# Key-row tiles, job loads and the first denominators re-placed, and TensorE's instructions issued in program order

## The chip, the cores and the metric

The kernel runs on one core of a Trainium2 chip. The metric is the device time of one execution in microseconds (us); for a kernel several executions are timed and the median is used. A core has TensorE (PE, matrix products into eight PSUM banks), VectorE (DVE), ScalarE (ACT), GpSimd (POOL) and SyncE (SP), each with an instruction queue of its own that is worked through in order, and DMA queues; here SyncE issues nearly all loads and GpSimd most stores.

## The reference

x is 2048 x 1024, all in float32. A linear-attention block (32 heads of 32) and a gated MLP are both applied to the normalised x, and the output is x plus one times the silu of the other:

```python
xn = layernorm(x)                                   # 2048 x 1024
q, k, v = xn @ wqkv                                 # 1024 x 3072, 32 heads of 32
phi = lambda t: where(t > 0, t + 1, exp(t)) + 1e-6
kv  = einsum("bhsd,bhse->bhde", phi(k), v);  z = phi(k).sum over tokens
o   = (phi(q) @ kv) / (phi(q) . z + 1e-6)
s   = o.reshape(2048, 1024) @ wo
b   = (silu(xn @ w1) * (xn @ w3)) @ w2              # 1024 -> 3584 -> 1024
out = x + s * silu(b)
```

## The kernel before

Precision comes from splitting every operand into a high and a low part (`split`, L89 to 96: ScalarE writes the high part, L93, VectorE the low one, L94) and three matmuls per product (`mm3`, L98 to 103). A matmul has a 128 x 128 weight tile and 512 columns. All large products use a Strassen-Winograd scheme: seven products (B11, T2, T3, T1, B21, T4, B22, each with a partner on the left: A11, S2, S3, S1, A12, A22, S4) in place of eight, joined by additions of VectorE from PSUM.

The tokens are worked in two halves (`half(h)`, L644). The order of the program is:

- first half: the rows of x are normalised and turned into the left operands (`prepare_first`, `prepare_rest`), then four key gemms, one for each pair of column blocks;
- four query gemms and 28 pairs of gate and up gemms, whose hidden values go to DRAM;
- second half: its left operands are loaded (they were made meanwhile), then four key gemms, the first two of which run product by product side by side (L686); then `row_products` (L548), which multiplies x transposed by the keys of all tokens in 28 steps of two times twelve matmuls, reading x and key rows back from DRAM (x_d, y_d) and leaving four blocks g_d; then the query, gate and up gemms of the second half;
- an attention segment (letter s in tile names) and five layers B0 to B4 of the down projection over 2, 3, 3, 3 and 3 pairs of hidden blocks (letter B in tile names). Each walks over eight groups of tokens. The first group, and the last before another layer, have the block index k outside and the seven products inside, in seven banks at once (`outer`, L1026); while the last group runs, the next layer's operands and weights are split between its k steps. The last layer multiplies by s and adds x (`finish`, L1178).

Side work is cut into small steps in Python generators. A gemm has seven products of twelve matmuls and calls `catch_up` (L412) six times, after a product each. `catch_up` takes first what lies in the list `later` (the turns and sums of key rows, below), and else one step of the first generator in `jobs`. In the first half's query, gate and up gemms this is `next_work` (L781): `prepare_next`, which normalises and turns the second half's rows in four blocks of 27 steps, and then 28 `weight_sums` jobs of three steps, which sum weights of the down projection. With the four steps that `later` takes there are 188 places for 192 steps, and what is left runs at the half's end. In the second half it is `attention_work` (L956): `spread_z` and the `denominators` of the first half's token blocks, then key-value products (`key_values`, L886, from g_d) and their merging with wo (`merge_wo`), then the `divide` jobs (L855), the second half's denominators and more divides. A divide loads queries and reciprocals, lets three steps pass, then multiplies (L873) and makes four sums on VectorE. `go_on` (L817) loads two jobs ahead; all job tiles are of tag "job" in one ring of three places.

A key gemm hands each finished quarter to `use` (L515) in `key_rows`: `phi` (L495 to 499: two ScalarE activations, then one VectorE instruction), and then `later` gets the turn: four transposes of TensorE into a bank (L505) and a copy out by ScalarE (L506). The rows go to pair tiles of the "b" ring (`pb`, eight places), which also holds the split weight products, the splits of the row products and spread z.

No order is written out by hand except where `issue_after` ties an instruction behind another. The framework plans every engine's instruction order from a modelled timeline (L1285): whichever instruction it expects to be ready is put first, on TensorE too, so the order on an engine can differ from that of the program.

Of the kernel before, what the change touches and what calls it, by code (L numbers as in the profile page):

```python
# [16 lines left out]
P = 128  # L17
C = 512
# [4 lines left out]
def tile_linear_attention_times_swiglu(  # L23
# [21 lines left out]


    const = ctx.enter_context(tc.tile_pool(name="const", bufs=1))
    dram = ctx.enter_context(tc.tile_pool(name="dram", bufs=1, space=DRAM))
# [49 lines left out]
    def mm3(acc, w, a, start, stop):  # L98

        (wh, wl), (ah, al) = w, a  # L100
        nc.tensor.matmul(acc, lhsT=wh, rhs=ah, start=start, stop=False, skip_group_check=True)  # L101
        nc.tensor.matmul(acc, lhsT=wh, rhs=al, start=False, stop=False, skip_group_check=True)  # L102
        nc.tensor.matmul(acc, lhsT=wl, rhs=ah, start=False, stop=stop, skip_group_check=True)  # L103

# [15 lines left out]
    def job_tile(shape, name):  # L120
        return praw.tile(shape, F32, tag="job", bufs=3, name=name)

# [98 lines left out]
    def prepare_next(i):  # L221
# [8 lines left out]
        def steps(_):  # L230
# [26 lines left out]
            keep_rows(1, i, "A22", a22)  # L257
            g = st.tile([P, 2, C], F32, tag="xg", bufs=1, name=f"xg{i}")
            nc.gpsimd.tensor_add(out=g[:, 0], in0=a21, in1=a22)
            nc.gpsimd.tensor_sub(out=g[:, 1], in0=a11, in1=a21)  # L260
            yield True
            keep_rows(1, i, "S1", g.rearrange("p n c -> p (n c)"))
            for _ in range(3):
                yield True
            nc.gpsimd.tensor_sub(out=g[:, 0], in0=g[:, 0], in1=a11)
            nc.gpsimd.tensor_sub(out=g[:, 1], in0=a12, in1=g[:, 0])
            yield True
            keep_rows(1, i, "S2", g.rearrange("p n c -> p (n c)"))
            yield True
            p_ = turn("A11", a11)  # L270
            keep("A11", p_)
            nc.scalar.copy(out=a11, in_=p_)
            yield True
            p_ = turn("A21", a21)
            nc.scalar.copy(out=a21, in_=p_)
            yield True
# [234 lines left out]
    def key_rows(h, pair):  # L511
# [12 lines left out]
        def turn(n, c, pk):  # L524
            if (c, n) == (0, 0):
                t = rows[c, n] = small(f"y00_{h}_{pair}")
            else:
                if (1 - c, 1) not in pairs:
                    pairs[1 - c, 1] = pb.tile([P, 2, C], F32, tag="b", name=f"y{c}_{h}_{pair}")
                t = rows[c, n] = pairs[1 - c, 1][:, n if c else 0]  # L530
# [17 lines left out]
    def row_products():  # L548
# [39 lines left out]
        for at, s in enumerate(steps):  # L588
# [15 lines left out]
            for e, (x_, y_) in enumerate(split_.pop(s)):  # L604
                for m in M:
                    c = slice(m * P, (m + 1) * P)
                    mm3(b[m], (x_[:, 0, c], x_[:, 1, c]), (y_[:, 0], y_[:, 1]),
                        begins and e == 0 and not onto, ends and e == 1)
                    if ends and e == 1:
                        row_sums(i, m, b[m], u, v)  # L610
                catch_up()
                yield
# [31 lines left out]
    def half(h):  # L644
# [40 lines left out]
        else:  # L685
            side_by_side(keys(0, paired=True), keys(1, paired=True))  # L686
            for pair in range(2, ND // 2):
                run(keys(pair))
            for _ in row_products():
                pass  # L690
# [125 lines left out]

    def go_on(work):  # L817

        data = [j.load() for j in work[:2]]
        for i, j in enumerate(work):  # L820
            yield from j.steps(data[i])
            if i + 2 < len(work):
                data.append(work[i + 2].load())

# [30 lines left out]
    def divide(m, k):  # L855
# [14 lines left out]
        def steps(t):  # L870
            for _ in range(3):
                yield True
# [80 lines left out]
    def late_work():  # L953
        yield from go_on([divide(m, k) for m in range(LATE, S // (2 * P)) for k in range(ND // 2)])

    def attention_work():  # L956
        yield from spread_z()
        H0, H1 = range(NCH // 2), range(NCH // 2, NCH)
        work = [j for c in H0 for j in denominators(c)]
        for k in range(ND // 2):  # L960
# [4 lines left out]
        work += [divide(m, k) for m in range(NT * H1[0], LATE) for k in range(ND // 2)]  # L965
        yield from go_on(work)

# [321 lines left out]
```

## Time and profile before

| | us |
|---|---|
| median of three runs | 2396.59 |
| lowest, highest | 2396.53, 2399.76 |
| profiled execution | 2399.34 |
| its span | 2397.6 |

| engine | busy us | share of the span |
|---|---|---|
| TensorE, matmuls | 2315.7 | 97% |
| TensorE, weight loads | 1896.1 | 79% |
| VectorE | 1772.2 | 74% |
| ScalarE | 919.6 | 38% |
| GpSimd | 751.0 | 31% |

The span is what the profile covers; the execution's own time is 1.7 us longer. The profiled execution is one of its own, 2.75 us above the median of the timed ones. In the profile's rows PE is a matmul, PEld a weight load that runs beside matmuls, SPq and POOLq are the DMA issues of SyncE and GpSimd. L505 means line 505 of the kernel. A row of the timeline has the start in us, the duration in us, engine, line, operation, written tile <- read tiles, the shape, how many instructions were joined in the row, and in brackets how long the engine had been idle before it and what ended that. A name such as cg__11115 is a bank (a, b, c or d) of a gate (g), key (k), query (q) or up (u) gemm with a number. A row of the waits has the engine's wait, its releaser, and the total, the count and the longest in us.

### The profile page before, as it was taken

To read this page: it belongs to the slowest core of one execution; us is meant where nothing else is said; L and a number is where in the kernel's file an instruction comes from. 1 tells how busy PE (TensorE), PEld (TensorE's weight loads), DVE (VectorE), ACT (ScalarE), POOL (GpSimd) and SP (SyncE) were. 2 spreads that over 40 slices of the span, in tenths; PEclk is the share of its full clock that TensorE was granted. 3 is DMA by queue.
4 is the path that set the end of the run, shared out by engine and by line. 5 is a ranking of instruction groups with operands and counts; after the bars stand their busy time and mean duration, and the time that the engine had idled before them with its cause. 6 is when DMAs were issued, how large, how long until landed. Compare 5 with 4: busy or idle time off the path is not lost.

```text
span 2397.6 us, 30961 instructions
## 1 busy us (share of the span) xinstructions
PE 2315.7 (97%) x10368; PEld 1896.1 (79%) x10368; DVE 1772.2 (74%) x2781; ACT 919.6 (38%) x1639; POOL 751.0 (31%) x892
## 2 busy tenths in 40 slices
PE   6999999999999889999999899999999999999998
PEld 5888788888887778778888788877787888888876
DVE  8878888887887655576766677777855676767798
ACT  5555333433332444344333233223423543342433
POOL 5341534367875320211423434323321000000033
PEclk9999999999999999999999999999999999999999
DMA  6455455476669566754555555557876665766588
GB/s 237 150 171 185 152 177 185 158 227 198 220 226 355 184 195 211 241 176 141 170 169 171 186 178 184 172 166 215 268 235 210 195 208 157 234 201 187 185 262 262
DMA packets 354016, 479.70 MB, mean 200 GB/s; under 512 B 24144, under 2 KB 262736, under 8 KB 353744
## 3 DMA queue, kind: packets, MB, share of 16 engines
q1 hardware_dynamic: 316608, 359.20, 47.8%
q0 software_dynamic: 37248, 118.52, 14.7%
q8 instruction: 81, 1.33, 0.2%
q14 instruction: 79, 0.65, 0.1%
HBM read 308.81 MB, written 172.49 MB: 201 GB/s over the span
## 4 chain that ended last, share of the span: by engine, by line
PE 43%; issue 10%; DMA 7%; DVE 4%; POOL 3%; ACT 1%; SPq 0%; POOLq 0%; DVEq 0%; ACTq 0%
PE g L101 2%; PE g L102 2%; PE g L103 2%; DMA qd<-pq_d 1%; PE cB L101 1%; PE cB L103 1%; PE cB L102 1%; PE aB L101 1%; PE aB L102 1%; PE dB L101 1%; PE aB L103 1%; PE dB L103 1%; PE dB L102 1%; DMA qs_d<-qd 1%; DMA rA22B<-h_d 1%
## 5 line engine op out<-in xcount | busy, mean ns | idle before, releaser
L740 POOL DMA_DIRECT2D h_d<-sg x112 | 82.7, 739 | 272.4 <-DVE sg L736 223.5
L1056 POOL DMA_DIRECT2D u_d<-uB x32 | 17.3, 540 | 407.1 <-DVE uB L1039 381.1
L94 DVE TENSOR_TENSOR xy<-xy,xy 128x512 fp32r<-128x512 f32 x112 | 75.9, 720 | 69.5 <-ACT xy L93 69.2
L93 ACT CAST xy<-xy 128x512 fp32r<-128x512 f32 x112 | 63.9, 620 | 86.2 <-PE g L103 60.1
L102 PE MATMUL g<-xy,xy 128*128 128x512 f32 x224 | 88.5, 395 | 0.0
L103 PE MATMUL g<-xy,xy 128*128 128x512 f32 x224 | 88.1, 394 | 0.0
L101 PE MATMUL g<-xy,xy 128*128 128x512 f32 x224 | 83.0, 395 | 2.8 <-ACT xy L93 2.3
L1039 DVE TENSOR_TENSOR acc<-cB,acc 128x512 f32<-128x512 f32 x50 | 34.3, 687 | 41.0 <-PE cB L103 41.0
L509 POOL DMA_DIRECT2D y_d<-y x40 | 29.7, 751 | 102.5 <-ACT y L506 79.7
L1039 DVE TENSOR_TENSOR acc<-dB,acc 128x512 f32<-128x512 f32 x56 | 38.5, 687 | 29.8 <-PE dB L103 29.6
L877 POOL DMA_DIRECT2D qs_d<-qd x32 | 17.9, 560 | 132.2 <-DVE qd L873 122.2
L722 POOL TENSOR_TENSOR hs<-sg 128x256 f32<-128x256 f32 x56 | 57.0, 1017 | 0.0
L720 POOL TENSOR_TENSOR hs<-hs,sg 128x256 f32<-128x256 f32 x56 | 56.4, 1008 | 0.1
L723 POOL TENSOR_TENSOR hs<-sg,hs 128x256 f32<-128x256 f32 x56 | 55.5, 992 | 1.6
L873 DVE SCALAR_TENSOR_TENSOR qd<-qd 128x512 f32<-128x512 f32 x32 | 21.9, 684 | 42.4 <-DMA qd<-pq_d 42.4
L101 PEld LDWEIGHTS g<-xy,xy 128*128 128x128 f32 x224 | 42.2, 189 | 12.5 <-ACT xy L93 2.9
L719 POOL TENSOR_TENSOR hs<-sg,sg 128x256 f32<-128x256 f32 x56 | 50.0, 892 | 1.2
L698 POOL DMA_DIRECT2D pq_d<-pq x32 | 17.4, 545 | 104.7 <-DVE pq L499 104.7
L102 PEld LDWEIGHTS g<-xy,xy 128*128 128x128 f32 x224 | 42.9, 192 | 9.0
L103 PEld LDWEIGHTS g<-xy,xy 128*128 128x128 f32 x224 | 42.9, 192 | 9.0
L748 POOL DMA_DIRECT2D h_d<-hs x60 | 45.9, 766 | 3.7 <-POOL hs L723 2.1
L755 POOL TENSOR_TENSOR w<-w 128x256 f32<-128x256 f32 x28 | 26.7, 955 | 58.5 <-DMA w<-in_B_w 58.5
(5311 smaller groups left out, 8383.7 us busy)
## 6 DMA issues: line engine op xcount, KB each, us to landing
h_d<-hs POOLq DMA_DIRECT2D x60, 256.0 KB, 3.3
h_d<-sg POOLq DMA_DIRECT2D x56, 256.0 KB, 3.5
w<-in_B_w SPq DMA_DIRECT2D x56, 256.0 KB
wt_d<-w SPq DMA_DIRECT2D x28, 512.0 KB
xy<-x_d SPq DMA_DIRECT2D x28, 512.0 KB
xy<-y_d SPq DMA_DIRECT2D x28, 512.0 KB
h_d<-hs SPq DMA_DIRECT2D x52, 256.0 KB
qs_d<-qd POOLq DMA_DIRECT2D x32, 384.0 KB, 4.6
```

What stands on the lines that cost most here:

```text
L93: nc.scalar.copy(out=hi, in_=src)
L94: return nc.vector.tensor_sub(out=lo, in0=src, in1=hi.bitcast(F32))
L101: nc.tensor.matmul(acc, lhsT=wh, rhs=ah, start=start, stop=False, skip_group_check=True)
L102: nc.tensor.matmul(acc, lhsT=wh, rhs=al, start=False, stop=False, skip_group_check=True)
L103: nc.tensor.matmul(acc, lhsT=wl, rhs=ah, start=False, stop=stop, skip_group_check=True)
L719: e.tensor_add(out=s1, in0=a21, in1=a22)
L720: e.tensor_sub(out=s2, in0=s1, in1=a11)
L722: e.tensor_sub(out=s3, in0=a11, in1=a21)
L723: e.tensor_sub(out=s4, in0=a12, in1=s2)
L740: nc.gpsimd.dma_start(out=h_d[i][2 * h + c][:, 2 * n:4 * n + 2, k], in_=src)
L748: queue.dma_start(out=h_d[i][2 * h + c][:, 6 + 4 * e:10 + 4 * e, k], in_=o[e].rearrange("p (e s) -> p e s", s=P))
L1039: return V.tensor_add(out=c, in0=src, in1=c)
```

## The change

- TensorE is taken out of the planner: `manual_schedule` over the whole kernel makes its instructions issue in the order of the program. The other engines are planned as before.
- The ring of job tiles has four places in place of three. `go_on` takes how many jobs to load ahead; `attention_work` asks for three.
- `prepare_next` turns A21 earlier, in the steps after the first sums, and holds its sums g in the job ring; it has 24 steps in place of 27, in each of four blocks.
- The key rows' pair tiles come from the job ring in place of the b ring.
- In `row_products` what `catch_up` issues is tied behind the last matmul of the twelve before it (for this `mm3` returns its last matmul).
- `spread_z` and the first half's denominators (one and 16 steps) are a job of their own, `first_denominators`, put ahead of the row products, and so run in their steps; `attention_work` begins with the key-value products.
- A divide lets four steps pass in place of three, except for the last two groups of tokens.

```diff
+    ctx.enter_context(tc.manual_schedule(engines={mybir.EngineType.PE}))
     const = ctx.enter_context(tc.tile_pool(name="const", bufs=1))
...
-        nc.tensor.matmul(acc, lhsT=wl, rhs=ah, start=False, stop=stop, skip_group_check=True)
+        return nc.tensor.matmul(acc, lhsT=wl, rhs=ah, start=False, stop=stop, skip_group_check=True)
...
-        return praw.tile(shape, F32, tag="job", bufs=3, name=name)
+        return praw.tile(shape, F32, tag="job", bufs=4, name=name)
...
-            g = st.tile([P, 2, C], F32, tag="xg", bufs=1, name=f"xg{i}")
+            g = job_tile([P, 2, C], f"xg{i}")
             nc.gpsimd.tensor_add(out=g[:, 0], in0=a21, in1=a22)
             nc.gpsimd.tensor_sub(out=g[:, 1], in0=a11, in1=a21)
             yield True
             keep_rows(1, i, "S1", g.rearrange("p n c -> p (n c)"))
-            for _ in range(3):
-                yield True
+            p_ = turn("A21", a21)
+            nc.scalar.copy(out=a21, in_=p_)
+            yield True
+            yield True
             nc.gpsimd.tensor_sub(out=g[:, 0], in0=g[:, 0], in1=a11)
             nc.gpsimd.tensor_sub(out=g[:, 1], in0=a12, in1=g[:, 0])
             yield True
             keep_rows(1, i, "S2", g.rearrange("p n c -> p (n c)"))
-            yield True
             p_ = turn("A11", a11)
             keep("A11", p_)
             nc.scalar.copy(out=a11, in_=p_)
-            yield True
-            p_ = turn("A21", a21)
-            nc.scalar.copy(out=a21, in_=p_)
             yield True
...
-                    pairs[1 - c, 1] = pb.tile([P, 2, C], F32, tag="b", name=f"y{c}_{h}_{pair}")
+                    pairs[1 - c, 1] = job_tile([P, 2, C], f"y{c}_{h}_{pair}")
...
-                    mm3(b[m], (x_[:, 0, c], x_[:, 1, c]), (y_[:, 0], y_[:, 1]),
-                        begins and e == 0 and not onto, ends and e == 1)
+                    last = mm3(b[m], (x_[:, 0, c], x_[:, 1, c]), (y_[:, 0], y_[:, 1]),
+                               begins and e == 0 and not onto, ends and e == 1)
                     if ends and e == 1:
                         row_sums(i, m, b[m], u, v)
-                catch_up()
+                with tc.issue_after(last.ins):
+                    catch_up()
                 yield
...
+            jobs.append((first_denominators(), False))
             for _ in row_products():
                 pass
...
-    def go_on(work):
+    def go_on(work, ahead=2):
 
-        data = [j.load() for j in work[:2]]
+        data = [j.load() for j in work[:ahead]]
         for i, j in enumerate(work):
             yield from j.steps(data[i])
-            if i + 2 < len(work):
-                data.append(work[i + 2].load())
+            if i + ahead < len(work):
+                data.append(work[i + ahead].load())
...
-            for _ in range(3):
+            for _ in range(4 if m < LATE else 3):
                 yield True
...
+    H0, H1 = range(NCH // 2), range(NCH // 2, NCH)
+
+    def first_denominators():
+        yield from spread_z()
+        yield from go_on([j for c in H0 for j in denominators(c)])
+
     def attention_work():
-        yield from spread_z()
-        H0, H1 = range(NCH // 2), range(NCH // 2, NCH)
-        work = [j for c in H0 for j in denominators(c)]
+        work = []
...
-        yield from go_on(work)
+        yield from go_on(work, 3)
```

## The prediction

> **What bounds the kernel now.** I read the page's sums first, then busy time by stage, then TensorE's waits, then the timeline round each.
>
> ```profile
> span 2397.6 us, 30961 instructions
> PE 2315.7 (97%) x10368; PEld 1896.1 (79%) x10368; DVE 1772.2 (74%) x2781; ACT 919.6 (38%) x1639; POOL 751.0 (31%) x892
> ```
>
> TensorE is busy for 97%, so what can be won or lost is its pauses. The stages, in columns of window, length, PE, PEld, DVE, ACT, POOL, granted clock, DMA share and GB/s:
>
> ```profile
> 766.00:862.00 96.00, 83.18 (x387) 67.69 (x386) 59.27 (x107) 43.68 (x79) 33.66 (x38) 0.96 0.59 195
> 862.00:1004.00 142.00, 141.55 (x625) 116.82 (x624) 77.76 (x117) 61.70 (x109) 20.75 (x22) 1.00 0.71 232
> 1004.00:1022.00 18.00, 14.99 (x72) 11.35 (x71) 13.29 (x31) 6.82 (x12) 4.53 (x5) 0.91 0.56 190
> 1340.00:1400.00 60.00, 53.16 (x228) 43.27 (x227) 43.88 (x80) 16.29 (x28) 18.92 (x25) 0.94 0.56 177
> 1840.00:1875.00 35.00, 31.55 (x133) 24.15 (x132) 27.29 (x50) 22.80 (x48) 2.70 (x5) 1.00 0.84 272
> 1875.00:2036.00 161.00, 161.00 (x712) 133.37 (x711) 102.59 (x188) 68.56 (x139) 6.49 (x12) 1.00 0.57 175
> 2036.00:2064.00 28.00, 28.00 (x125) 23.18 (x124) 27.03 (x49) 12.67 (x25) 1.62 (x3) 1.00 0.84 271
> 2265.00:2398.00 133.00, 119.17 (x512) 96.10 (x511) 118.03 (x196) 49.26 (x94) 38.91 (x43) 0.96 0.86 262
> ```
>
> Inside a layer TensorE never pauses: 712 matmuls in 161.00 us, 0.226 us each, which is the pace used below. It pauses in the second half's keys (766 to 862), at the row products' end, at 1374 and at some layer starts. At 2036 it doesn't pause although VectorE is full (27.03 of 28 us). The waits, as total, times, longest:
>
> ```profile
> PE trk L505 <- DVE pk L499: 11.7, 4, 6.7
> PE cg__11115 L101 <- DVE c22g__11150 L462: 6.2, 1, 6.2
> PE g L101 <- ACT xy L93: 2.3, 1, 2.3
> PE bk__6485 L101 <- ACT T2k__6324 L93: 2.0, 1, 2.0
> PE cg__13351 L101 <- DVE c22g__13386 L462: 1.8, 1, 1.8
> ...
> PE aq__8368 L101 <- ACT uq__8367 L439: 0.7, 1, 0.7
> ```
>
> **Gains.** *The divide* (waits one step more, loads three jobs ahead out of four places).
>
> ```profile
> 1363.97 0.69 DVE L873 SCALAR_TENSOR_TENSOR qd<-qd 128x512 f32<-128x512 f32 x1 [7.58 <-DMA qd<-pq_d]
> 1374.01 0.80 PE L101 MATMUL cg__11115<-A,T4g__11153 128*128 128x512 f32 x1 [6.24 <-DVE c22g__11150 L462]
> L101 PE MATMUL cg__11115<-A,T4g__11153 x4: 389/545/796, 1374.0 to 1377.5; 128*128 128x512 f32 x4
> ```
>
> VectorE stands 7.58 us before a divide whose rows haven't landed; behind it in its queue is the sum that frees the bank for cg__11115, and TensorE loses 6.24 us, then some 1.7 in a slow restart (545 ns where steady matmuls have 389). One step more (one product, 12 x 0.226 = 2.7 us) and one job more ahead (five steps, 13.6 us) cover 7.58. With cg__13351's 1.8 this is 9.7: −10. Ends: −11, and −4 if the sixteen later divides meet the same lateness with only the longer wait.
>
> *The row products' end and the first keys of the second half.*
>
> ```profile
> 1007.52 1.52 PE L101 MATMUL g<-xy,xy 128*128 128x512 f32 x4 [2.33 <-ACT xy L93]
> 1008.84 0.63 PE L102 MATMUL g<-xy,xy 128*128 128x512 f32 x1
> 740.97 4.91 SPq L776 DMA_DIRECT2D wt_d<-w  x1
> 760.41 0.50 PE L101 MATMUL bk__6485<-S,T2k__6324 128*128 128x512 f32 x1 [2.04 <-ACT T2k__6324 L93]
> 762.27 0.64 PE L103 MATMUL bk__6485<-S,T2k__6324 128*128 128x512 f32 x1 [1.14 <-DVE T2k__6324 L94]
> ```
>
> In 1004 to 1022, 18.00 − 14.99 = 3 us are lost: the last steps' splits wait behind other work. With the b ring freed of four key-row tiles a pair this can go: −3 (0 to −4). At 740.97 the stores of the left-over weight sums (192 steps for 188 places) still stand in SyncE's queue ahead of the second half's loads. The change's 27 − 24 = 3 steps less, four times, lets all fit (180 for 188): of 2.04 + 1.14 and some 2 of slow restart I take −2.5 (0 to −5). Another 0.7 is the first query gemm's wait for its copy (last line of the waits): ScalarE and VectorE then no longer spread z beside it. Gains: −16 (−5 to −21).
>
> **Losses.** *Key rows in program order.* At present the planner puts the four transposes of a key tile wherever they are ready. In program order they stand directly behind the product whose result they turn (nine times in the second half: three turns each of pairs 0 and 1, run side by side, and of pair 3; pair 2 has a product between, through the queue `later` left over). TensorE then waits for this chain:
>
> ```profile
> 842.01 0.69 DVE L468 TENSOR_TENSOR c22k__7036<-dk__7002,c22k__7036 128x512 f32<-128x512 f32 x1 [2.03 <-PE dk__7002 L103]
> 842.74 0.63 ACT L497 ACTIVATE pk<-c22k__7036 128x512 f32<-128x512 f32 x1 [5.57 <-DVE c22k__7036 L468]
> 843.27 0.58 ACT L497 ACTIVATE pk<-ak__6979 128x512 f32<-128x512 f32 x1
> 843.75 1.14 ACT L498 ACTIVATE pk<-pk 128x512 f32<-128x512 f32 x2
> 844.41 0.69 DVE L499 SCALAR_TENSOR_TENSOR pk<-c22k__7036,pk 128x512 f32<-128x512 f32 x1 [1.70 <-ACT pk L498]
> 778.81 1.28 ACT L498 ACT_TABLE_LOAD   x1
> 784.67 0.60 PE L505 MATMUL trk<-ident,pk 128*128 128x128 f32 x4
> ```
>
> From the product's end (842.01) to the turn's input (844.41 + 0.69 = 845.10) it is 3.1 us; without the other tile's 0.5 in between 2.6; with a table load of 1.28 more, 4.4 at most; the turns that have no sum ahead (n = c = 0) 2.3. Six of 2.9, three of 2.3 and one table load: 17.4 + 6.9 + 1.3 = 25.6. The stage already loses 96.00 − 83.18 = 12.8, and the waits for L499 (11.7) are these same chains, so I count the difference: +13. Ends: 0, if the waits only move, and +26, if the present ones stay too. The first half's three later pairs have a product between (2.72 for 3.1): +1.
>
> *Layer starts.* A layer's first tokens run with k outside, so its first 21 matmuls want all seven left operands. At present the planner runs on with ready k's of others:
>
> ```profile
> 2038.16 0.39 PE L101 MATMUL B11B<-B,XA11B 128*128 128x512 f32 x1
> 2041.14 0.55 DVE L94 TENSOR_TENSOR XS3B<-rS3B,XS3B 128x384 fp32r<-128x384 f32 x1
> 2049.02 0.55 DVE L94 TENSOR_TENSOR XS4B<-rS4B,XS4B 128x384 fp32r<-128x384 f32 x1
> 2052.44 0.39 PE L101 MATMUL aB<-B,XA11B 128*128 128x512 f32 x1
> ```
>
> XS4B's low half is there at 2049.57. In program order B22 is the seventh product and wants it 18 matmuls after 2038.2, at 2042.2; behind it 45 matmuls stand before aB: 2049.57 + 45 x 0.226 = 2059.7, against 2052.44. That is +7.3 at most, where VectorE keeps its order. VectorE is full, so it can pull the split forward only by leaving sums for later: 2 at the least. I take 5 for each of the two starts of this kind (B2, B3), 2.5 for B0 and B1 (at 1840 to 1875, 35.00 − 31.55 = 3.45 are lost already) and 2 for the last layer, where VectorE has 118.03 of 133: +17 (8 to 27).
>
> *The first key-value product* moves up to the second place of the first query gemm, as nothing stands ahead of it.
>
> ```profile
> 1018.90 0.54 POOL L622 DMA_DIRECT2D g_d<-gc x1 [1.05 <-DVE eps L802]
> DMA to landing us min/median/max: 2.3/4.1/8.5
> 1061.74 0.52 SPq L892 DMA_DIRECT2D gw<-g_d  x1
> L847 DVE RECIPROCAL r<-r 128x512 f32<-128x512 f32 x4 | 13.4, 3344 | 0.0
> ```
>
> Its g rows are issued at 1018.90, the landings (second line) take 4.1 in the median, and I count the load back the same: 1027.1. TensorE is at that place 24 matmuls after the 1014.7 at which the gemm starts, 1020.2, where today the load isn't issued before 1061.74. Up to 6.9 (10 with the longest landing); other issues drift too: +5 (0 to 10). The denominators moved into the row products cost two RECIPROCALs of 3.34 us on a VectorE that has 142.00 − 77.76 = 64 us to spare there, but in two blocks ahead of splits, and one of eight b places: +1.5 (0 to 4; TensorE has 141.55 of 142.00 there, so there is nothing to win). Their matmuls are the same ones, moved; their eight loads on SyncE and two stores on POOL go past the row products' own, at a DMA share of 0.71 that leaves room. A job's step there is now tied behind the twelve matmuls that it follows: at nothing, as 142.00 − 20.75 us of POOL and the 64 of VectorE take it up; without that cover each of the 56 places could hold a split by one such operation, 0.7, which the 4 above bounds. The gaps between the rearranged turns of the next rows (one product instead of none or two) and xg in the ring have the same answer: the jobs have a product's 2.7 us for a step of about one, so nothing; with loads late in a full ring it would be a wait as long as a landing, 4.
>
> *Slow restarts.* A pause of 2.33 us at 1007.52 was followed by matmuls of 0.63 us, some 2 us lost. Of the new waits, the kv one and one other: +4 (0 if none, +24 if a dozen).
>
> The Trainium skill ("TensorE: Matmul & The Clock Gate", Part 1: The HAM clock gate, The two states) says that the clock is halved only after an idle window of about 3.4 us. By that rule the turns' waits of 2.3 to 2.9 never slow the clock and this term would be 2, the sum 2 lower. The trace disagrees: it has the halved pace after 2.33 us at 1007.52. The measurement decides.
>
> **Sum.** Losses 13 + 1 + 17 + 5 + 1.5 + 4 = +41.5, gains −16.2, net +25.3. The profiled execution took 2399.34, so the changed one 2424.6; the runs' median stands 2.75 lower (2396.59), so 2422. Its own range is 2407 to 2440. 0.2%, about what a measurement of this kernel tells from no change, is 4.8 us: faster is under 2391.8, slower over 2401.4.
>
> **Rivals.** *A, the other side: the other engines are planned round a TensorE in order.* The splits and key chains that TensorE needs next get priority, so turns and layer starts cost what they cost now, and the gains decide: 2396.59 − 16 = 2380. For it: ScalarE is free (43.68 of 96.00 in the keys) and only chains matter. Against it: the chain of 3.1 us has no other work in it but 0.5. It decides where turns, layer starts and restarts together stay under some 10 us. Chance 0.16.
>
> *B, a slow restart after nearly every new wait:* twelve at 2 in place of two, +20: 2442, with 8 more for the turns 2450. For it 1007.52; against it the waits in the keys, where the stage's clock is still 0.96. Chance 0.13.
>
> *C, waits only move:* the turns cost no more than the 12.8 of today and the layer starts 8: 25.3 − 13 − 9 − 4 = −1, so about 2396 to 2400. Chance 0.10, nearly all of it within 0.2%. That program order changes nothing can't be: with XS4B missing until 2049.57 TensorE had no pause from 2036 to 2064, and in program order its 18th matmul of the layer needs it.
>
> *The forecast* keeps 0.61. Slower: forecast, B and a little of C, 0.75; same 0.09; faster 0.16. The range leaves out A, which is all below 2392, and the little above B's 2448: 2394 to 2448, some 0.18 left out.
>
> **What would show it.** Right: four-matmul transposes in the keys each with an idle of 2 to 3 us behind L499; at layer starts, B22 with an idle before it behind XS4B; no idle of 6 us at cg; the divides without 7.58. Wrong: a key stage (96 us) with no more than 13 idle; layer starts without pauses; a kv product with none; a new long wait of TensorE on a load of a job, which I have at nothing, as three jobs ahead of at least two steps give it some 16 us (six products of 2.7).

## The result, and the profile after

The changed kernel takes 2492.15 us (median), the kernel before beside it 2398.18: the ratio is 1.0389, with a 95% interval from 1.0369 to 1.0409. That is 94 us slower, where +25 was forecast, and outside the range of 2394 to 2448. The profiled execution took 2490.27. One of the four executions of e11_order_mended (2593.20, the profiled one) was in a slower state, which its ratio below leaves out and its median doesn't.

The page of the changed kernel:

```profile
span 2488.3 us, 30990 instructions
PE 2351.6 (95%) x10368; PEld 1914.3 (77%) x10368; DVE 1799.3 (72%) x2781; ACT 921.9 (37%) x1637; POOL 747.6 (30%) x892
```

The first thing to see is that TensorE's busy time rose by 35.9 us (2351.6 for 2315.7) for the same 10368 matmuls. The span rose by 90.7, so 54.8 us are new pauses, and 35.9 are matmuls that took longer. Counted in the two traces, some 27 of the 35.9 are matmuls that followed one another more slowly, at half clock nearly all; some 6 are the last matmuls ahead of a pause, which are busy for their whole 0.39 us where one in a row counts 0.226. In the clock record of the traces, the kernel before has ten stretches at half clock, the changed one 24 (56.7 and 117.8 us in all), and full clock in between; the mean clock falls from 0.989 to 0.977.

Busy time by stage says where. Each stage runs from its own first matmul to the next stage's. The stages are, in this order: first half's keys, first half's gate and up gemms, second half's keys, second half's query gemms, layers; columns as in the prediction. First the kernel before, then the changed one:

```profile
11.50:127.40 115.90, 104.51 (x505) 86.43 (x505) 102.05 (x183) 64.77 (x114) 48.92 (x53) 0.94 0.53 177
...
206.50:752.80 546.30, 541.78 (x2402) 447.15 (x2402) 449.80 (x579) 193.21 (x326) 302.67 (x345) 1.00 0.63 203
752.80:855.70 102.90, 86.91 (x397) 70.09 (x396) 71.20 (x119) 47.65 (x86) 42.11 (x47) 0.96 0.65 221
...
1014.70:1101.20 86.50, 85.83 (x436) 66.13 (x436) 65.17 (x102) 39.73 (x68) 10.83 (x20) 1.00 0.53 173
...
1842.50:2397.60 555.10, 538.21 (x2353) 441.25 (x2351) 407.03 (x709) 220.17 (x432) 56.20 (x75) 0.99 0.68 212
```

```profile
11.30:136.80 125.50, 107.92 (x504) 88.40 (x505) 107.63 (x182) 63.21 (x114) 54.62 (x59) 0.93 0.50 167
...
215.90:778.20 562.30, 545.86 (x2401) 449.24 (x2400) 458.16 (x576) 191.70 (x325) 310.05 (x355) 0.99 0.62 201
778.20:910.00 131.80, 98.49 (x397) 77.12 (x396) 69.57 (x115) 50.19 (x85) 33.73 (x39) 0.90 0.43 145
...
1075.70:1172.00 96.30, 87.61 (x397) 72.92 (x396) 63.74 (x98) 43.46 (x77) 15.74 (x22) 0.95 0.54 176
...
1899.80:2488.30 588.50, 554.64 (x2353) 446.84 (x2351) 409.37 (x709) 221.71 (x432) 54.40 (x75) 0.97 0.65 200
```

| stage | longer by, us | of it pauses | of it longer busy |
|---|---|---|---|
| first half's keys | 9.6 | 6.2 | 3.4 |
| first half's gate and up gemms | 16.0 | 11.9 | 4.1 |
| second half's keys | 28.9 | 17.3 | 11.6 |
| second half's query gemms | 9.8 | 8.0 | 1.8 |
| layers | 33.4 | 17.0 | 16.4 |

A pause is the stage's length less its busy time. (The query stage has 39 matmuls less than before, as denominators left it and key-value products came, so its split is a rough one.) The other stages together are 6.8 shorter: the row products are 6.7 longer with 79 matmuls more, the second half's gate and up gemms and the attention segment together 13.5 shorter.

The chief waits of TensorE after:

```profile
PE trk L504 <- DVE pk L498: 35.4, 14, 4.6
PE tA L163 <- DVE v L147: 11.3, 1, 11.3
PE kv L903 <- DMA gw<-g_d: 8.7, 1, 8.7
PE cg__13351 L102 <- DVE c22g__13381 L461: 7.4, 1, 7.4
PE T4B L104 <- DVE XA22B L95: 4.9, 4, 1.5
```

The key turns' wait (11.7 us in 4 before, all in the second half) is now 35.4 in 14, of which 31.0 in 11 are in the second half. The wait of 6.2 at cg__11115 is gone, but cg__13351, later in the same gemms, has 7.4 for 1.8.

### The profile page after: what moved, and what is told of

It reads as the page before. It is cut to its first block, busy times and chain, and to the rows that moved or that the text cites. A ratio compares the mean times of both kernels' runs of the same rounds, so it can differ in the third digit from the quotient of the medians.

```text
span 2488.3 us, 30990 instructions
## 1 busy us (share of the span) xinstructions
PE 2351.6 (95%) x10368; PEld 1914.3 (77%) x10368; DVE 1799.3 (72%) x2781; ACT 921.9 (37%) x1637; POOL 747.6 (30%) x892
## 4 chain that ended last, share of the span: by engine, by line
PE 67%; DVE 11%; DMA 7%; issue 4%; ACT 3%; POOL 1%; SPq 0%; POOLq 0%; ACTq 0%; DVEq 0%
PE g L102 2%; PE g L104 2%; PE g L103 2%; PE cB L102 1%; PE cB L103 1%; PE cB L104 1%; PE dB L103 1%; PE dB L102 1%; PE dB L104 1%; PE aB L103 1%; PE aB L102 1%; PE aB L104 1%; DMA qs_d<-qd 1%; DVE sg L737 1%; PE bB L103 1%
## 5 line engine op out<-in xcount | busy, mean ns | idle before, releaser
L1061 POOL DMA_DIRECT2D u_d<-uB x32 | 17.3, 541 | 430.6 <-DVE uB L1044 389.1
L102 PE MATMUL g<-xy,xy 128*128 128x512 f32 x224 | 89.2, 398 | 0.0
L103 PE MATMUL g<-xy,xy 128*128 128x512 f32 x224 | 87.8, 392 | 0.2 <-DVE xy L95 0.2
L104 PE MATMUL g<-xy,xy 128*128 128x512 f32 x224 | 87.7, 392 | 0.0
L504 PE MATMUL trk<-ident,pk 128*128 128x128 f32 x128 | 22.3, 303 | 35.4 <-DVE pk L498 35.4
L102 PEld LDWEIGHTS g<-xy,xy 128*128 128x128 f32 x224 | 42.4, 189 | 12.6 <-issue 2.9
L504 PEld LDWEIGHTS trk<-ident,pk 128*128 128x128 f32 x128 | 16.4, 153 | 44.0 <-DVE pk L498 41.5
L103 PEld LDWEIGHTS g<-xy,xy 128*128 128x128 f32 x224 | 42.4, 189 | 9.2 <-DVE xy L95 0.7
```

Source lines behind the costliest of these rows:

```text
L104: return nc.tensor.matmul(acc, lhsT=wl, rhs=ah, start=False, stop=stop, skip_group_check=True)
```

## The experiments

All ratios are to the kernel before, run beside each. Stages are of the profiled execution, which need not lie at the median: e1_planned's took 2428.80, 8 us above its median, e13_sums_on_vector's 5 above, e6_kv_later's 4 below. So differences of a few us between two stages are rough.

| kernel | median us | ratio, 95% interval |
|---|---|---|
| the change | 2492.15 | 1.0389 (1.0369 to 1.0409) |
| e1_planned | 2420.37 | 1.0097 (1.0076 to 1.0118) |
| e2_order_only | 2467.50 | 1.0295 (1.0275 to 1.0315) |
| e3_lag | 2461.04 | 1.0268 (1.0245 to 1.0291) |
| e4_layers_planned | 2460.43 | 1.0264 (1.0245 to 1.0284) |
| e5_old_turns | 2413.29 | 1.0071 (1.0056 to 1.0086) |
| e6_kv_later | 2401.78 | 1.0020 (1.0011 to 1.0030) |
| e7_regions | 2395.37 | 0.9990 (0.9980 to 0.9999) |
| e8_products_outside | 2468.05 | 1.0301 (1.0270 to 1.0331) |
| e9_extra_step | 2404.00 | 1.0029 (1.0017 to 1.0041) |
| e10_keys_region | 2393.81 | 0.9991 (0.9980 to 1.0001) |
| e11_order_mended | 2420.02 | 1.0079 (1.0059 to 1.0100) |
| e12_late_turn | 2388.81 | 0.9965 (0.9955 to 0.9976) |
| e13_sums_on_vector | 2408.88 | 1.0045 (1.0029 to 1.0062) |
| e14_sums_late_turn | 2378.73 | 0.9923 (0.9909 to 0.9937) |

**The two halves of the change.** e1_planned is the change without its first line, e2_order_only the kernel before with that line alone.

```diff
 e1_planned (on the change)
-    ctx.enter_context(tc.manual_schedule(engines={mybir.EngineType.PE}))
 e2_order_only (on the kernel before)
+    ctx.enter_context(tc.manual_schedule(engines={mybir.EngineType.PE}))
```

> The change without its first part: TensorE's order is planned as before, all other parts stay. Theory O (program order makes the whole loss, the other parts gain the 16 us of the prediction): about 2382. Rival P (a good part of the loss comes from the moved work: the A21 turn, the key-value products at the front of the query gemms, the key rows in the job ring): 2420 to 2450.

> The kernel before with TensorE's instructions in program order and nothing else. Theory O: about 2505, the 2492 of the change without its 16 us of gains. Rival P: 2440 to 2470. By stage, theory O has the first half's gate and up gemms lose as much as in the change (some 16 us); if the moved A21 turn were the cause there, this kernel would lose nothing in that stage.

Program order alone costs 70 us (2467.50 − 2397.36), the other parts alone 23 (2420.37 − 2397.36), and 70 + 23 = 93 is the 94 of the change. So theory O fell: the other parts, from which I had expected a gain of 16, lose 23. By stage e2_order_only has the second half's keys at 134.3 us, the layers 31 us longer, and the second half's query, gate and up gemms 17 longer, but its first half's gate and up gemms take 544.4 us, no longer than before (546.2); e1_planned has these at 567.4. The loss in the gate gemms comes from the other parts, the losses in keys and layers from the order.

**The key turns.** e3_lag is the change, with `catch_up` taking from `later` only what was put there before its previous call, and the turn of Y10 forced ahead of the row products, which read it.

```diff
-        if later:
-            later.pop(0)()
+        calls[0] += 1
+        if later and later[0][0] < calls[0] - 1:
+            later.pop(0)[1]()
...
+            while len(later) > 1:
+                later.pop(0)[1]()
             jobs.append((first_denominators(), False))
```

> The change, but a key tile's turn is taken from the list one call later than it is now, so at least one product of 2.7 us stands between a tile's product and its transposes. Theory O by its chains (3.1 us from product to turn, and a slow restart after it): the second half's keys lose some 20 to 29 us of their 29, the first half's some 5: about 2460. Rival (the waits only move behind the next product, since VectorE and ScalarE are what is short there): above 2480.

It is 31.1 us faster than the change. The keys gain more (39 us in the second half, 7 in the first); 10 are lost again in the first half's gate and up gemms (572.4 for 562.3), for a reason that wasn't looked for, and 4 in the row products. The first wait of the stage in the changed kernel's timeline shows what was taken away:

```profile
800.89 0.69 DVE L467 TENSOR_TENSOR c22k__6539<-dk__6489,c22k__6539 128x512 f32<-128x512 f32 x1 [1.37 <-PE dk__6489 L104]
801.66 0.63 ACT L496 ACTIVATE pk<-c22k__6539 128x512 f32<-128x512 f32 x1 [2.87 <-DVE c22k__6539 L467]
802.31 1.28 ACT L497 ACT_TABLE_LOAD   x1
803.60 0.63 ACT L497 ACTIVATE pk<-pk 128x512 f32<-128x512 f32 x1
804.32 0.69 DVE L498 SCALAR_TENSOR_TENSOR pk<-c22k__6539,pk 128x512 f32<-128x512 f32 x1 [2.74 <-ACT pk L497]
805.08 0.66 PE L504 MATMUL trk<-ident,pk 128*128 128x128 f32 x4 [4.22 <-DVE pk L498]
805.49 0.48 PE L102 MATMUL dk__6509<-S,T1k__6413 128*128 128x512 f32 x1
...
806.45 0.63 PE L102 MATMUL dk__6509<-S,T1k__6413 128*128 128x512 f32 x1
806.88 0.63 PE L103 MATMUL dk__6509<-S,T1k__6413 128*128 128x512 f32 x1
```

The chain is the one of the prediction, link by link, with its one table load, and nothing else stands in it. Behind it the matmuls take 0.63 us, one every 0.43, until the clock is back. One wait of the stage is longer than its chain, at pair 2's turn, which has a product ahead of it:

```profile
862.17 4.64 DVE L95 TENSOR_TENSOR T1k__6861<-wk__6582,T1k__6861 128x512 fp32r<-128x512 f32 x1
866.73 0.68 DVE L467 TENSOR_TENSOR c22k__6859<-dk__6821,c22k__6859 128x512 f32<-128x512 f32 x1
870.19 0.66 PE L504 MATMUL trk<-ident,pk 128*128 128x128 f32 x4 [4.57 <-DVE pk L498]
```

The sum that begins the chain stands behind a split of VectorE of 4.64 us, beside which GpSimd adds key rows. With one product more in between, waits and stage of e3_lag are:

```profile
PE trk L505 <- DVE pk L499: 4.4, 3, 2.6
```

```profile
781.40:874.30 92.90, 86.45 (x398) 69.52 (x396) 69.69 (x115) 47.84 (x85) 32.83 (x37) 0.98 0.59 199
```

The stage takes 92.9 us, ten less than in the kernel before, with the pauses and the slow matmuls gone together (98.49 to 86.45 busy); e1_planned, with the other parts but the planner's order, has 99.2 there.

**The layer starts.** e4_layers_planned ends the region of program order behind the attention segment. e8_products_outside keeps program order and changes the loops of the first token group of each layer.

```diff
 e4_layers_planned
     era1.close()
+    order.close()
 e8_products_outside
+                if m == 0 and self.name != "s":
+                    for n in PRODUCTS:
+                        self.product(b[n], X, n, ks)
+                else:
                     for k in ks:
                         for n in PRODUCTS:
                             self.product(b[n], X, n, [k])
```

> The change, but program order holds only up to the end of the attention segment; the five layers are planned as before. Theory O: the 32 us that the layers lost come back: about 2460. Rival (VectorE is late at the layer starts whoever sets TensorE's order, because of what the other parts leave behind): above 2480.

> The change with the first token group of each layer taking its seven products one after the other, all k of each, in place of all seven for each k; same matmuls, same seven banks. If the layer starts lose because all seven left operands are wanted within 21 matmuls (4.8 us) while VectorE owes some 18 us of splits and sums there: the layers lose 10 to 18 us less, 2475 to 2482. If the weights' last splits are what is waited for: no better than 2492, or worse, since the first product then wants them at once.

They are 31.7 and 24.1 us faster than the change; with the planner's order the layers take 558.1 us, 3 more than before. A layer start in the changed kernel:

```profile
2105.78 0.55 DVE L95 TENSOR_TENSOR XS3B<-rS3B,XS3B 128x384 fp32r<-128x384 f32 x1
...
2106.38 0.69 PE L104 MATMUL T3B<-T,XS3B 128*128 128x512 f32 x1 [1.47 <-DVE XS3B L95]
...
2107.30 0.63 PE L103 MATMUL T1B<-T,XS1B 128*128 128x512 f32 x1
...
2112.58 0.55 DVE L95 TENSOR_TENSOR XA22B<-rA22B,XA22B 128x384 fp32r<-128x384 f32 x1
...
2113.19 0.68 PE L104 MATMUL T4B<-T,XA22B 128*128 128x512 f32 x1 [1.47 <-DVE XA22B L95]
```

VectorE works without a pause there, at splits of the operands in turn with splits of the weights and sums of the seven banks, and TensorE takes one operand after the other as it gets ready: a wait of about 1.5, a few matmuls at the slow pace, the next wait. When a product takes all its k at once, an operand is wanted every 9 matmuls in place of every 3 (in a layer of three pairs), and VectorE keeps up. The layers' stage is then, in e8_products_outside:

```profile
1901.90:2469.80 567.90, 541.32 (x2353) 443.60 (x2351) 409.91 (x709) 222.22 (x432) 53.75 (x75) 0.98 0.68 207
```

The stage is 20.6 us shorter, 13.3 of them busy time (554.64 to 541.32). So the order in which the operands are wanted makes some 60% of the price of the layer starts (20.6 of 33.4), and about half of the price is slow matmuls. What stays, 12.8, is in the main waits elsewhere: 5.33 at the start of B0, for its weights (B11B at 1909.52), and 2.66 and 2.78 for sums in the last layer.

**The other parts, undone one by one.** e5_old_turns is e1_planned with prepare_next's steps as before (27 steps, A21 turned after A11; the sums stay in the job ring). e6_kv_later is e5_old_turns with the second block's denominators back ahead of the key-value products.

```diff
 e5_old_turns (on e1_planned)
-            p_ = turn("A21", a21)
-            nc.scalar.copy(out=a21, in_=p_)
-            yield True
-            yield True
+            for _ in range(3):
+                yield True
...
+            yield True
             p_ = turn("A11", a11)
...
+            yield True
+            p_ = turn("A21", a21)
+            nc.scalar.copy(out=a21, in_=p_)
 e6_kv_later (on e5_old_turns)
-        yield from go_on([j for c in H0 for j in denominators(c)])
+        yield from go_on(denominators(0))
 
     def attention_work():
-        work = []
+        work = denominators(1)
```

> e1_planned with the steps of prepare_next as in the kernel before (27 steps, A21 turned after A11); its sums stay in the job ring. If the moved A21 turn makes the seven waits for the gate gemms' sums (21 us of the first half's gate and up gemms): about 2400. If the ring with the sums and the key rows makes them: 2418 to 2422, with the waits where they were.

> e5_old_turns with the denominators of the second token block left where the kernel before has them, ahead of the key-value products, so that the first of these comes eight steps (some 22 us) later. If the first key-value product waits only for the way of g through DRAM: some 5 us under e5_old_turns. If it waits for its place in the job ring or in a queue: no faster than e5_old_turns.

e5_old_turns is 7 us faster only. Its first half's gate and up gemms lose nothing any more (543.2 us for 567.4), but 192 steps don't fit into 188 places, and the second half's keys go from 99.2 to 105.9 us and the row products from 165.2 to 167.7. (That is 15 of the 17 us between the two profiled executions; between the medians it is 7.) The end of the left-over weight sums, a gain of the prediction, is thus real. e6_kv_later is another 11.5 us faster, more than the 5 expected. Its product doesn't wait any more and the query stage is 3.7 us shorter; the rest is spread over other stages, the row products (5.1, with eight steps fewer) and the second half's gate and up gemms (3.7) first. In the changed kernel the first key-value product had waited like this (the last store of g, the load, the product):

```profile
1081.59 0.54 POOL L622 DMA_DIRECT2D g_d<-gc  x1 [1.26 <-DVE gc L641]
1084.97 1.20 SPq L893 DMA_DIRECT2D gw<-g_d  x2
1090.00 2.07 PE L903 MATMUL kv<-gw 128*128 128x128 f32 x8 [8.69 <-DMA gw<-g_d]
```

From the store to the product it is 8.4 us, as estimated (8.2); TensorE was there 8.7 us early.

**Where the point of meeting and GpSimd come in.** Why do the gate gemms lose? e9_extra_step has the new steps of prepare_next with one idle step more (25 in place of 24) on e6_kv_later. e12_late_turn, on e10_keys_region, has 25 steps too, but A21 turned late, as before. e13_sums_on_vector is e1_planned with prepare_next's four sums on VectorE.

```diff
 e9_extra_step (on e6_kv_later, with the change's steps of prepare_next)
+            yield True
             a11, a12, a21, a22 = (t[c][:, n * C:(n + 1) * C] for c in range(2) for n in range(2))
 e12_late_turn (prepare_next of the kernel before, sums in the job ring)
-            for _ in range(3):
-                yield True
+            yield True
 e13_sums_on_vector
-            nc.gpsimd.tensor_add(out=g[:, 0], in0=a21, in1=a22)
-            nc.gpsimd.tensor_sub(out=g[:, 1], in0=a11, in1=a21)
+            nc.vector.tensor_add(out=g[:, 0], in0=a21, in1=a22)
+            nc.vector.tensor_sub(out=g[:, 1], in0=a11, in1=a21)
...
```

> e6_kv_later with the changed steps of prepare_next (A21 turned early), but one idle step more ahead of its sums: 25 steps for a block of rows in place of 24. 24 is four gemms of six steps, so that in the change every block meets the gate gemms at the same point. If this point is what costs (seven waits of 21 us): most of them go, and with 184 steps for 188 places the left-over weight sums go from the second half's keys too (some 7 us): 2393 to 2398. If the early A21 turn costs by itself: 2412 to 2420.

> e10_keys_region with prepare_next as in the kernel before but for two of its idle steps: A21 is turned after A11, and a block has 25 steps as in e10_keys_region. If the place of the A21 turn costs: the gate and up gemms of the first half go from 553.7 to some 545 us and the kernel to about 2385. If only the point at which the blocks meet the gemms counts: 553 us, 2394.

> e1_planned with the four sums of each block in prepare_next on VectorE in place of GpSimd. If VectorE is late in the gate gemms because its instructions are drawn out while GpSimd adds (0.68 us alone, up to 4.77 beside the sums): the seven waits shrink by half or more, -10 to -18, 2402 to 2410. If VectorE is late because it has too much to do or in the wrong order: 11 us more work on it leaves the waits or makes them longer, 2420 or more.

The stage takes 567.4 us with 24 steps and the early turn, 553.5 with 25 (e9_extra_step; 553.7 in e10_keys_region), 551.8 with 25 and the late turn, 543.2 with 27. So the place of the A21 turn counts for some 2 us in this stage (the whole kernel is 5 faster, between the two forecasts), and the number of steps, which sets where a block meets the gemms, for most. The keys do gain from the steps that fit (97.6 us in e9_extra_step for 105.5), but the two cancel, and e9_extra_step is no faster than e6_kv_later (2404.00 for 2401.78).

With 24 steps, which are four gemms of six (a half has 28 gate and up gemms, in 14 pairs), the blocks of e1_planned meet the same place again and again:

```profile
PE cg__2328 L101 <- DVE c22g__2366 L460: 3.8, 1, 3.8
PE cg__3620 L101 <- DVE c22g__3658 L460: 3.8, 1, 3.8
PE cg__2974 L101 <- DVE c22g__3012 L460: 3.8, 1, 3.8
```

These waits end at 266.80 (cg__2328), 352.47 (cg__2974) and 439.75 (cg__3620), four gemms apart. What happens there:

```profile
262.31 2.17 DVE L94 TENSOR_TENSOR T2u__2344<-wu__2129,T2u__2344 128x512 fp32r<-128x512 f32 x1 [0.74 <-ACT T2u__2344 L93]
...
263.86 1.73 POOL L267 TENSOR_TENSOR xg<-xg,xn 128x512 f32<-128x512 f32 x1
264.51 1.63 DVE L342 TENSOR_TENSOR wu__2129<-wu__2129 128x512 f32<-128x512 f32 x1
...
266.07 0.68 DVE L460 TENSOR_TENSOR c22g__2366<-cg__2328,ug__2302 128x512 f32<-128x512 f32 x1
...
266.80 0.69 PE L101 MATMUL cg__2328<-A,T4g__2241 128*128 128x512 f32 x1 [3.81 <-DVE c22g__2366 L460]
...
267.29 0.63 PE L102 MATMUL cg__2328<-A,T4g__2241 128*128 128x512 f32 x1
```

TensorE waits for VectorE's sum that frees the bank. That sum takes its 0.68 us, but the two instructions ahead of it take 2.17 and 1.63, while GpSimd adds. The same split and sum without the block's sums on GpSimd, in e13_sums_on_vector, in the same place:

```profile
259.32 0.69 DVE L94 TENSOR_TENSOR T2u__2344<-wu__2129,T2u__2344 128x512 fp32r<-128x512 f32 x1 [0.74 <-ACT T2u__2344 L93]
259.93 0.68 DVE L460 TENSOR_TENSOR c22g__2366<-cg__2328,ug__2302 128x512 f32<-128x512 f32 x1
...
262.88 0.68 DVE L267 TENSOR_TENSOR xg<-xg,xn 128x512 f32<-128x512 f32 x1
```

The split takes 0.69, and the subtraction (L342) now stands behind the sum; so the order on VectorE has changed as well as the duration. In e1_planned there are six such waits (four of some 4 us and two of 1.8; the seven of the expectations were a miscount). Three of those of 3.8 are gone here, though VectorE has 16 instructions more; the stage takes 554.3 us and the kernel is 11.5 us faster than e1_planned. Three waits of 2.3 to 4.9 us stay in it.

> e12_late_turn with the four sums of each block of prepare_next on VectorE, as in e13_sums_on_vector. Its first half's gate and up gemms still lose some 12 us (3.7, 2.8 and 1.8 us at single waits, and slow restarts). If these too come from VectorE drawn out beside GpSimd: 8 to 10 us less, about 2380. If the place of the waits only moves with the load: within 3 us of 2389.

e14_sums_late_turn has the same sums on VectorE in e12_late_turn. Its gate and up gemms take 540.9 us (551.8), and all of it 2378.73: the forecast of 2380 held. Their stage has no pause left to speak of:

```profile
209.30:750.20 540.90, 539.76 (x2402) 446.06 (x2401) 450.41 (x588) 191.96 (x323) 288.66 (x340) 1.00 0.64 208
```

**Program order in some stages, and everywhere with its waits mended.** e7_regions is e6_kv_later with program order (and the later turn) in the second half's keys and program order in the attention segment. e10_keys_region is e9_extra_step with the keys alone. e11_order_mended is the change with the edits of e3_lag, e8_products_outside, e6_kv_later (the denominators) and the idle step of e9_extra_step.

```diff
 e7_regions and e10_keys_region
+            lag[0] = True
+            with tc.manual_schedule(engines={mybir.EngineType.PE}):
                 side_by_side(keys(0, paired=True), keys(1, paired=True))
                 for pair in range(2, ND // 2):
                     run(keys(pair))
+                while len(later) > 1:
+                    later.pop(0)[1]()
+            lag[0] = False
 e7_regions
-    run(attention, ahead=ask_first)
+    with tc.manual_schedule(engines={mybir.EngineType.PE}):
+        run(attention, ahead=ask_first)
```

> e6_kv_later with TensorE in program order in two stages only: the second half's keys, with each turn one call later as in e3_lag, and the attention segment. By the stages of e3_lag against e1_planned (keys 92.9 for 99.2 us, attention 161.8 for 170.2) some 14 us under e6_kv_later. Rival: the gain of these stages was work moved into their neighbours (row products and query gemms were 4 us longer each there), then within 5 us of e6_kv_later.

> e9_extra_step with TensorE in program order in the second half's keys alone, each turn one call later. In e7_regions keys and row products together took 262.7 us for the 268.1 of e6_kv_later, and the attention segment 3.6 us more: some 4 us under e9_extra_step. Rival: with no left-over sums at its start the stage has nothing to gain from it: within 2 us of e9_extra_step.

> The change, all of TensorE still in program order, with four edits together: each turn one call later (e3_lag, -31.1), the first token group of a layer product by product (e8_products_outside, -24.1), the second block's denominators ahead of the key-value products (-11.5 as in e6_kv_later) and the idle step of e9_extra_step (-15 to -20). If these four places carry the loss and are independent: 2405 to 2412. If program order costs by itself, wherever it is relieved: above 2425.

e7_regions is 6.4 us faster than e6_kv_later, less than half of what was expected: keys and row products took 5.4 us less, but the attention segment 3.6 more (176.9 for 173.3). Program order with the later turn in the second half's keys alone gains 10 us (e10_keys_region against e9_extra_step), more than the 4 expected: keys 92.1 for 97.6, row products 156.6 for 162.0. The later turn in the planner's order wasn't tried, so it isn't shown which of the two gains this.

e11_order_mended has a ratio of 1.0079 (about 2416 us): four local edits take back 76 of the 94 us, with TensorE in program order throughout. It missed its 2405 to 2412 by a little. Where the rest lies stays open.

e12_late_turn (0.9965) and e14_sums_late_turn (0.9923, 0.9909 to 0.9937) are faster than both kernels. e14_sums_late_turn is the change without program order but in the second half's keys, with the turns one call later, the second denominators in their old place, 25 steps in prepare_next with the late A21 turn, and its sums on VectorE.

## Why the prediction was wrong

The sign was right, and most places were named; the size was 94 for 25. By its own steps:

- *Slow restarts: +4, measured some 27.* This is the step that failed by most. I gave two of a dozen waits a slow restart; the clock record has 14 more stretches at half clock (24 for 10). Two us for each was about right (27 over 14), the count was wrong. With the ends of matmuls ahead of pauses, which I had nowhere, TensorE's busy time rose by 35.9 us: 11.6 in the second half's keys, 16.4 in the layers, the rest in the first half and the query gemms. Rival B named the mechanism and came near its size (24), and I held the stage's clock of 0.96 against it, which in a stage of 103 us already stood for 4 us. After, it is 0.90.
- On the rule of the Trainium skill ("TensorE: Matmul & The Clock Gate", Part 1: The HAM clock gate, The two states), that an idle window of some 3.4 us halves the clock: the layer starts of this kernel have the halved pace behind waits of 1.47 us (2106.38, then 0.63 at 2107.30), one close on another. The measurement decides: a run of short waits is enough here.
- *Key rows: +13, measured +17.3 of pauses in the second half* (33.3 for 16.0). The links of the chain were as taken, and the 11.7 of present waits did go, as credited. But ten turns waited, 30.8 us in all, where I had nine and 25.6: pair 2's turn, which I had covered by its product, waited 4.57 behind the split of 4.64 us. *First half +1, measured 9.6 with its restarts*; e3_lag has 7.5 of it back (118.1 for 125.6).
- *Layer starts: +17, measured 17.0 of pauses.* Place and size were right, and that VectorE's splits are waited for. But the sign that I named, B22 waiting for XS4B's low half, isn't among the waits: they are several of 1.0 to 1.5 us, most at T3 and T4. The start of B2 has 4.0 and that of B3 3.8 for the 5 of each; that the total agrees so well is in part luck. The 16.4 of longer busy time belong to the step above.
- *Key-value product: +5 (up to 10), measured a wait of 8.7*, in the upper half of its bounds; e6_kv_later, with all that moves with it, gains 11.5.
- *The divide: −10, measured about nothing.* VectorE's waits before divides fall from 42.4 us in 9 to 22.9 in 5, and the 6.24 at cg__11115 is gone; but cg__13351 now waits 7.4 (until 1713.46) for 1.8, behind divides that still stand before their loads, this one and one with 1.43 at 1709.32:

```profile
1695.73 0.69 DVE L874 SCALAR_TENSOR_TENSOR qd<-qd 128x512 f32<-128x512 f32 x1 [5.15 <-DMA qd<-pq_d]
```

  So the gain was below the low end of the term (−4, "if the sixteen later divides meet the same lateness"). That the later place is due to the change of step itself wasn't tried; e6_kv_later, in which the divides meet the gemms eight steps later, has no wait there, but one of 3.2 at an earlier up gemm.
- *The row products' end: −3, measured nothing* (pauses of 2.95 in the stage for 2.78). With program order alone, in e2_order_only, the stage has 0.13, so this wait can go without the places in the b ring.
- *The left-over weight sums: −2.5, measured 6.7 to 8 in the keys alone* (105.9 to 99.2, 105.5 to 97.6).
- *The steps of prepare_next: nothing, measured 16 in the change* and 21 to 24 in e1_planned (567.4 for 546.2 and 543.2). This is the second step that failed. I covered a moved step by the 2.7 us of a product, for a step of about one. Two things were left out: VectorE's instructions with two inputs in SBUF are drawn out while GpSimd adds, which the kernel before has too, and with 24 steps the blocks meet the gemms at the same bad point.

Rival A (the other engines planned round an ordered TensorE) is refuted: where program order put a turn behind its product, TensorE waited for the whole chain. Rival C (waits only move) is too: the second half's turns wait 31.0 us for 11.7.

## What to carry to other kernels

Before an engine is set to the program's order, look for every instruction whose input is made from the result directly ahead of it, and move it behind other work first: a lag of one product turned a loss of 29 us in the keys into a gain of 10 (6 of it against e1_planned). A pause of TensorE is not priced by its length alone: count the matmuls behind it at half pace, also behind pauses of 1.5 us if they come close together. A step of side work that is free by its sum may still collide with its neighbours; where GpSimd and VectorE both work from SBUF, price VectorE by its durations beside GpSimd's work.

## What the runs showed of the hardware

VectorE's instructions with both inputs in SBUF are, in the mean, drawn out when GpSimd adds beside them, those with one input in a bank aren't. In e1_planned, first half's gate gemms, grouped by line (count, busy us, mean ns, idle):

```profile
L342 DVE TENSOR_TENSOR wu__4386<-wu__4386 128x512 f32<-128x512 f32 x4 | 5.4, 1340 | 0.1
...
L342 DVE TENSOR_TENSOR wg__4237<-wg__4237 128x512 f32<-128x512 f32 x4 | 2.8, 692 | 0.1
```

The same four subtractions take 1340 ns in an up gemm's weights, while GpSimd sums hidden values, and 692 in a gate gemm's, while it doesn't. The sum L460, one of whose inputs is a bank, takes 0.68 us beside a subtraction of GpSimd (L758):

```profile
482.15 2.12 DVE L342 TENSOR_TENSOR wu__3755<-wu__3755 128x512 f32<-128x512 f32 x1
483.67 1.18 POOL L758 TENSOR_TENSOR w<-w 128x256 f32<-128x256 f32 x1
484.20 0.68 DVE L460 TENSOR_TENSOR c22g__3982<-cg__3948,ug__3926 128x512 f32<-128x512 f32 x1
```

Over the whole stage of e1_planned, 139 additions, subtractions and multiplications of VectorE (128x512) with both inputs in SBUF lay beside GpSimd's for most of their time: they took 1.36 us in the mean and up to 3.74, and the 211 with none beside them at most 0.70. The 58 with a bank input that lay beside GpSimd's took at most 0.69. The Trainium skill ("SBUF — State Buffer", Who interferes with whom) says the same: a VectorE instruction with two SBUF inputs contends with GpSimd's reads, one with at most one SBUF input doesn't. The runs agree, with twice the duration in the mean.

The other surprise is the share of the clock: of 91 us, some 27 were matmuls at half pace, and of the 38.9 and 20.6 us that e3_lag and e8_products_outside gain in their stages, 12.0 and 13.3 are busy time of the same matmuls.
